# Which queue issues the key and value loads: batch 12's second halves and batch 18 go from GpSimd to SyncE

## The chip, the cores and the metric

The kernel runs on one core of a Trainium2 chip. The metric is device microseconds of one execution. TensorE is called PE here (PEld is its weight load), VectorE DVE, ScalarE ACT, GpSimd POOL and SyncE SP. SP and POOL issue all transfers: what SP issues goes through queue q1, what POOL issues through queue q0, and both run on the same 16 DMA engines.

## The reference

A retention layer (a linear recurrence, 4 batches of 8 heads, 768 steps, head size 64) is followed by a feed-forward layer with squared ReLU.

```
gamma = 1.0 - 2.0 ** (-5.0 - np.arange(H))
for t in range(S):
    state = gamma * state + einsum('bhd,bhe->bhde', k[:, :, t], v[:, :, t])
    y[:, :, t] = scale * einsum('bhd,bhde->bhe', q[:, :, t], state)
x = y.transpose(0, 2, 1, 3).reshape(3072, 512)
h = maximum(x @ w_in, 0)          # 512 -> 2048
out = h * h @ w_out               # 2048 -> 512
```

Inputs and outputs are float32.

## The kernel before

**Chunks.** The 768 steps of a batch are cut into 6 chunks of 128, 24 chunks over all batches. A batch is named by its first chunk: batch 6 is chunks 6 to 11, batch 12 is chunks 12 to 17, batch 18 is chunks 18 to 23. For each chunk the kernel multiplies keys by queries, masks the scores, multiplies them by the values, and carries a state from chunk to chunk. The result of one or more chunks (a block: first four chunks, then two each) is the x of the feed-forward layer, whose two products are most of PE's work.

**The order** is written out by hand. `pieces()` yields the feed-forward products of all blocks, a piece at a time, and after piece n the function `before(n)` emits what `put(n, ...)` has placed there. A place is thus a position in the program, not a time. From chunk 12 on, chunk m ends at place d = 70 + 8 (m - 10), and a place takes about 0.93 us in the profile. Each engine works through its own instructions in this order, so an instruction that waits holds up all behind it on its engine.

**Half form.** Chunks 8 to 23 take a form in which two half chunks lie above each other in the 128 partitions (`attend2`). For chunk m with end d:

- `dma_transpose_q` (L425, place d - 16, even chunks): SP transposes the scaled queries of two chunks by DMA into qT.
- `cast_k2` (L658, place d - 18): POOL casts the keys from the staging tile to ks_bdp.
- `transpose_k2` (L681, place d - 13): SP transposes ks_bdp by DMA into kT. Two kT buffers and two ks_bdp buffers take turns.
- `scale_v2` (L667 on DVE, L675 on POOL, place d - 9): values times a table of decays, kf2.
- `scores2` (L697, place d - 5): PE reads kT and qT. `state2` (L724) and `outputs2` (L746, L753) follow.

The table kf2 and the mask of the half form are made by `pack_constants` in two steps, at places 22 and 38; the second step is two operations of DVE (L202, L203) and one of ACT (L284).

**Loads.** `load_q` (L105) fetches the queries of two chunks, 512 KB, on SP. The keys and values of a whole batch are fetched by `batch_loads` (L147) into a staging tile, 64 partitions, one head and `size` chunks at a time, in runs of 64 floats. Batch 6's rest (chunks 8 to 11) comes by SP in 8 issues of 4 chunks for the keys and 8 for the values, 128 KB each. Batches 12 and 18 come by POOL in 16 issues of 3 chunks each, 96 KB: first the eight head loads of the first three chunks (the first half), then those of the last three (the second half). `places` says at which place each issue stands. Four staging buffers serve all of it; batch 18 takes those of chunks 8 to 11.

**SP's queue** from 78 us on, for every two chunks: kT, kT, two stores of results (L886, L888, which wait for DVE), the query load, qT, and again. The stores' tiles have four buffers.

Of the kernel before, what the change touches and what calls it, by code (L numbers as in the profile page):

```python
# [28 lines left out]
def kernel(  # L29
# [9 lines left out]
    nc = tc.nc  # L39
# [87 lines left out]
    def stage_tile(size):  # L127
        t = stage.tile([P, 2 * NCH * NPAIR * D], FP32, name="stage")
        return t[:, 0:size]
# [3 lines left out]
    def batch_loads(m, name, size):  # L133


        b, i = chunks[m]
        src, to = (k, raw_k) if name == "k" else (v, raw_v)
        t = kept_tiles.pop((m, name), None)
        if t is None:
            t = stage_tile(2 * NCH * NPAIR * D)  # L140
        t = t.rearrange("s (p w d) -> s p w d", p=NPAIR, d=D)
        for j in range(NCH - i):
            to[m + j] = t[:, :, 2 * j : 2 * j + 2].rearrange("s p u d -> s u p d")
        for w in range(0, NCH - i, size):
            for hh, rows in enumerate(halves):
                for p in range(NPAIR):
                    (nc.sync if m == 8 else nc.gpsimd).dma_start(  # L147
                        t[rows, p, 2 * w : 2 * (w + size)],
                        src[b, 2 * p + hh, (i + w) * C : (i + w + size) * C].rearrange(
                            "(w s) d -> s w d", s=64  # L150
                        ),
                    )
                    yield
# [110 lines left out]
    def pack_constants():  # L264
        lng2 = const.tile([P, 2, NPAIR], FP32)
        for hh, rows in enumerate(halves):
            for p in range(NPAIR):
                nc.gpsimd.memset(lng2[rows, :, p : p + 1], float(np.log(gammas[2 * p + hh])))
        logs = lng2.rearrange("s u p -> s (u p)")
        scaled = exponents([[C, NCH], [C // 2, 2], [0, NPAIR]], 1, "ex_k2", logs, halves)  # L270
        nc.gpsimd.memset(cmask2[:], 0.0)
        for rows in halves:
            nc.gpsimd.affine_select(
                out=cmask2[rows],
                in_=cmask2[rows],
                compare_op=ALU.is_gt,
                fill=1.0,
                base=0,
                pattern=[[-1, 2], [-2, C // 4]],
                channel_multiplier=1,  # L280
            )
        yield
        ex = scaled()
        nc.scalar.activation(kf2.rearrange("s i u p -> s i (u p)"), ex[:], AF.Exp, scale=-1.0)  # L284
        yield
# [929 lines left out]
    def put(place, what, *args):  # L1215
        parts.setdefault(place, []).append((what, args))
# [69 lines left out]
        put(place, early_store, tb, which)  # L1286
    packed = pack_constants()
    put(22, next, packed)
    put(38, next, packed)
    for j, t in enumerate(ks_bd2s + v_bd2s + [s_bds[2]]):  # L1290
        for hh in range(2):
            put(24 + j, zero_off_diagonal, t, hh)
# [7 lines left out]
    for m, d in zip(range(PACK_FROM, NCHUNK), done):  # L1300
# [6 lines left out]
        (8, "v"): [33, 33, 34, 34, 35, 35, 36, 36],  # L1307
        (12, "k"): [49, 50, 51, 52, 53, 54, 55, 56] + [74 + j for j in range(8)],
        (12, "v"): [58, 59, 60, 61, 62, 64, 65, 66] + [82 + j for j in range(8)],
        (18, "k"): [92 + 4 * j // 3 for j in range(8)] + [117 + 4 * j // 3 for j in range(8)],  # L1310
        (18, "v"): [103 + 4 * j // 3 for j in range(8)] + [128 + 4 * j // 3 for j in range(8)],
    }
    for (m, name), at_places in places.items():
        loads = batch_loads(m, name, 4 if m == 8 else 3)
        for place in at_places:
            put(place, next, loads)

# [53 lines left out]
```

## Time and profile before

| | us |
|---|---|
| runs shown, median (lowest, highest) | 209.42 (207.17, 210.19) |
| the profiled execution, its own time | 208.36 |
| its span, first to last instruction | 206.6 |
| PE busy | 196.7 |
| DVE busy | 152.9 |
| ACT busy | 135.6 |
| POOL busy | 112.1 |
| POOL's issues at L147, 64 of 662 ns | 42.0 |
| share of 16 DMA engines' time, q1 (SP) and q0 (POOL) | 68.4%, 19.2% |

The table is read from the profile's page: the busy time of an engine is the sum of its instructions in that one execution, and its time outside the span (208.36 - 206.6) is start and end of the program. The share of a queue is the time that its packets took; packets of two queues overlap, so that shares of a stretch can add up to more than one. "Landing" in the views of transfers is the time from the issue to the completion. A line with a start and a duration of SP is the issue, not the transfer.

### The profile page before, as it was taken

How to read it: one execution, taken by the hardware profiler on the slowest of the kernel's cores; microseconds unless marked ns; L12 is line 12 of the kernel's file. 1: busy time of each engine (PE TensorE's matmuls, PEld its weight loads, DVE VectorE, ACT ScalarE, POOL GpSimd, SP SyncE). 2: the span in 40 equal slices, each digit the busy share in tenths (PEclk: the TensorE clock that was granted, in tenths of full speed). 3: DMA queues.
4: the chain of work that ended last, by engine and by line, in shares of the span. 5: the costliest groups of instructions: out<-in, count | busy, mean ns of one | idle time of the engine just before them, and what ended most of it. 6: DMA issues, size and time to landing. Idle time of an engine off the chain costs nothing.

```text
span 206.6 us, 5855 instructions
## 1 busy us (share of the span) xinstructions
PE 196.7 (95%) x2373; PEld 165.2 (80%) x2373; DVE 152.9 (74%) x305; ACT 135.6 (66%) x276; POOL 112.1 (54%) x198
## 2 busy tenths in 40 slices
PE   5889999999999999999999899999999999999993
PEld 1457644876888998789989699999989999898883
DVE  4687899498885678589697588598697797474374
ACT  8375885677943666693794595793785786874730
POOL 5332549823230768975999788779986226100000
PEclk9999999999999999999999999999999999999999
DMA  6999999999999999899699998799897551300202
GB/s 160 290 313 379 310 268 247 205 203 239 238 169 174 240 292 134 149 289 185 174 200 180 221 225 176 190 197 158 217 201 156 137 105 38 119 0 3 102 0 102
DMA packets 70730, 38.12 MB, mean 185 GB/s; under 512 B 43952, under 2 KB 64688, under 8 KB 70704
## 3 DMA queue, kind: packets, MB, share of 16 engines
q1 hardware_dynamic: 65520, 29.37, 68.4%
q0 software_dynamic: 5184, 8.39, 19.2%
q8 instruction: 18, 0.29, 0.6%
q14 instruction: 8, 0.07, 0.1%
HBM read 27.26 MB, written 6.29 MB: 162 GB/s over the span
## 4 chain that ended last, share of the span: by engine, by line
PE 69%; DMA 17%; POOL 4%; DVE 4%; ACT 2%; issue 1%; SPq 0%; DVEq 0%; ACTq 0%
PE psf L803 28%; PE psf L837 12%; PE tp L837 8%; DMA kT<-ks_bdp 7%; PE psf L1096 6%; DMA stage<-in_moe_w_in_dram 4%; DMA w_out_bf<-in_moe_w_out_dram 3%; PE psf L1002 3%; DMA kn<-in_k_dram 3%; POOL stage L147 2%; PE st L697 2%; POOL ks_bdp L658 2%; PE y L753 1%; PE y L746 1%; PE c_ps L724 1%
## 5 line engine op out<-in xcount | busy, mean ns | idle before, releaser
L803 PE MATMUL psf<-xt,w_in_bf 128*128 128x256 bf16 (+2 forms) x880 | 92.5, 259 | 0.4 <-DVE w_in_bf L336 0.3
L803 PEld LDWEIGHTS <-w_in_bf 128*128 128x128 bf16 x880 | 70.9, 98 | 11.2 <-DVE w_in_bf L336 0.7
L812 ACT ACTIVATE h<-psf 128x512 bf16<-128x512 f32 x96 | 56.2, 595 | 20.5 <-PE psf L803 20.0
L774 DVE TENSOR_TENSOR h<-h 128x512 bf16<-128x512 bf16 x72 | 31.8, 458 | 14.8 <-ACT h L812 14.6
L658 POOL CAST ks_bdp<-stage 64x512 bf16<-64x512 f32 x32 | 25.6, 799 | 20.6 <-issue 12.1
L675 POOL COPY v_bd<-v 64x512 bf16<-64x512 bf16 x32 | 20.6, 642 | 23.4 <-DVE v L667 22.2
L837 PEld LDWEIGHTS <-h 128*128 128x128 bf16 x288 | 26.3, 98 | 3.3 <-DVE h L774 0.6
L833 DVE TENSOR_TENSOR osb<-psf,u 128x256 f32<-128x256 f32 x34 | 13.7, 422 | 17.1 <-ACT u L878 9.9
L147 POOL DMA_DIRECT2D stage<-in_k_dram x32 | 21.0, 662 | 0.0
L147 POOL DMA_DIRECT2D stage<-in_v_dram x32 | 21.0, 662 | 0.0
L760 ACT ACTIVATE xt<-y 128x512 bf16<-128x512 f32 x16 | 12.0, 748 | 8.8 <-PE y L753 8.8
L366 DVE TENSOR_TENSOR qs<-qn,qf 128x512 bf16<-128x512 f32 x22 | 16.6, 758 | 1.1 <-DMA qn<-in_q_dram 1.1
L837 PEld LDWEIGHTS <-k_bd 128*128 128x128 bf16 x144 | 13.7, 98 | 1.8 <-issue 0.2
L772 ACT ACTIVATE h<-h 128x512 bf16<-128x512 bf16 x24 | 14.6, 626 | 0.5
L667 DVE TENSOR_TENSOR v<-stage,kf 128x512 bf16<-128x512 f32 x16 | 13.4, 838 | 0.0
L733 ACT ACTIVATE s_bd<-c_ps 64x256 bf16<-64x256 f32 x29 | 10.6, 367 | 3.4 <-PE c_ps L724 3.3
L704 DVE TENSOR_TENSOR pt<-st,cmask 128x512 bf16<-128x512 f32 x16 | 11.0, 687 | 2.4 <-PE st L697 1.9
L734 ACT ACTIVATE s_bd<-c_ps 64x256 bf16<-64x256 f32 x29 | 11.0, 378 | 0.4
L837 PE MATMUL tp<-w_out_bf,h 128*128 128x256 bf16 x72 | 11.2, 273 | 0.0
L334 POOL CAST w_in_bf<-stage 128x256 bf16<-128x256 f32 x14 | 6.1, 465 | 9.2 <-DMA stage<-in_moe_w_in_dram 9.2
L837 PE MATMUL psf<-w_sum,h 128*128 128x256 bf16 x72 | 10.8, 273 | 0.0
L833 DVE TENSOR_TENSOR k_bd<-h 128x512 bf16<-128x512 bf16 x18 | 10.4, 576 | 0.3
(146 smaller groups left out, 328.7 us busy)
## 6 DMA issues: line engine op xcount, KB each, us to landing
qn<-in_q_dram SPq DMA_DIRECT2D x12, 512.0 KB, 7.0
out_dram<-osb SPq DMA_DIRECT2D x23, 256.0 KB, 3.3
stage<-in_k_dram POOLq DMA_DIRECT2D x32, 96.0 KB, 4.5
stage<-in_v_dram POOLq DMA_DIRECT2D x32, 96.0 KB, 4.9
stage<-in_moe_w_in_dram SPq DMA_DIRECT2D x4, 512.0 KB, 6.9
stage<-in_moe_w_in_dram SPq DMA_DIRECT2D x2, 1024.0 KB, 10.9
w_out_bf<-in_moe_w_out_dram POOLq DMA_DIRECT2D x4, 512.0 KB, 9.5
kn<-in_k_dram SPq DMA_DIRECT2D x2, 512.0 KB, 6.4
```

The costliest lines, as they stand in the source:

```text
L147: (nc.sync if m == 8 else nc.gpsimd).dma_start(t[rows, p, 2 * w : 2 * (w + size)], src[b, 2 * p + hh, (i + w) * C : (i + w + size) * C].re ...
L366: engine.tensor_tensor(out=out, in0=by, in1=table[:, :, None].to_broadcast([P, H, D]), op=ALU.mult)
L658: nc.gpsimd.tensor_copy(ks[rows, :, hh, :].rearrange("s (u p) d -> s u p d", u=2), kn[rows])
L667: nc.vector.tensor_tensor(out=v2.rearrange("s (u p) d -> s u p d", u=2), in0=vn, in1=kf2[:, i, :, :, None].to_broadcast([P, 2, NPAIR, D]), ...
L675: nc.gpsimd.tensor_copy(v_bd[rows, :, hh, :], v2[rows])
L772: nc.scalar.activation(hv, hv, AF.Square)
L774: nc.vector.tensor_mul(hv, hv, hv)
L803: nc.tensor.matmul(hp, lhsT=w_in_bf[g][:, cb, fq * 128 : (fq + 1) * 128], rhs=xts[tb][:, cb, cols], start=(cb == 0), stop=(cb == NCB - 1),)
L812: nc.scalar.activation(hv, hp[:], AF.Relu)
L833: nc.vector.tensor_tensor(out=out, in0=in0, in1=in1, op=op)
L837: nc.tensor.matmul(to, lhsT=left[:, j], rhs=right(j) if callable(right) else right[:, j], start=(start and j == 0), stop=(stop and j == NF ...
L1096: nc.tensor.matmul(to[:], lhsT=left(j), rhs=right(j), start=(start and j == 0), stop=(j == NFB // 2 - 1), skip_group_check=True,)
```

## The change

Three edits. First, `batch_loads` now issues on POOL only the first half of batch 12 (w is 0), and all else on SP: the second half of batch 12 (8 loads of keys, 8 of values, 96 KB each, at the places they had) and batch 18. Second, batch 18 is fetched six chunks at a time: 8 loads of keys and 8 of values, 192 KB each, at every second place from 91 (keys) and 102 (values), instead of 32 loads of 96 KB between places 92 and 137. Third, the second step of `pack_constants` stands at place 42 instead of 38.

```diff
-                    (nc.sync if m == 8 else nc.gpsimd).dma_start(
+                    (nc.gpsimd if m == 12 and w == 0 else nc.sync).dma_start(
...
-    put(38, next, packed)
+    put(42, next, packed)
...
-        (18, "k"): [92 + 4 * j // 3 for j in range(8)] + [117 + 4 * j // 3 for j in range(8)],
-        (18, "v"): [103 + 4 * j // 3 for j in range(8)] + [128 + 4 * j // 3 for j in range(8)],
+        (18, "k"): [91 + 2 * j for j in range(8)],
+        (18, "v"): [102 + 2 * j for j in range(8)],
...
-        loads = batch_loads(m, name, 4 if m == 8 else 3)
+        loads = batch_loads(m, name, {8: 4, 12: 3, 18: 6}[m])
```

In the instruction order, POOL has 48 issues less and SP 32 more. On SP, seven key loads of batch 12 stand between kT 12 and kT 13; one key load and five value loads of it between kT 13 and qT 14, among two stores and the query load; three value loads between qT 14 and kT 14; one value load of batch 12 and three key loads of batch 18 between kT 14 and kT 15; three loads of batch 18 between kT 15 and qT 16, three between qT 16 and kT 16, five between kT 16 and kT 17, and the last two after kT 17. PE's instructions are the same, in the same order; on DVE and ACT only the table's three operations move.

## The prediction

> **What bounds the kernel now.** I read the engine shares first, then the waits of PE (TensorE), then the busy time stage by stage, then SP's (SyncE's) own queue and the landing time of single transfers.
>
> ```profile
> PE 196.7 (95%) x2373; PEld 165.2 (80%) x2373; DVE 152.9 (74%) x305; ACT 135.6 (66%) x276; POOL 112.1 (54%) x198
> ```
>
> PE is busy 196.7 of 206.6 us, so only its 9.9 idle us can be won by moving transfers. The stages say where they lie (columns: PE, PEld, DVE, ACT, POOL busy, granted clock, DMA share, GB/s):
>
> ```profile
> 60.00:75.00 15.00, 14.89 (x223) 13.82 (x221) 10.16 (x21) 9.15 (x21) 5.30 (x9) 1.00 1.09 224
> 75.00:90.00 15.00, 14.47 (x191) 12.86 (x189) 10.40 (x21) 10.59 (x23) 13.07 (x20) 1.00 1.08 182
> 90.00:105.00 15.00, 15.00 (x186) 13.40 (x182) 12.26 (x22) 10.19 (x22) 12.44 (x19) 1.00 1.02 203
> 105.00:120.00 15.00, 13.96 (x171) 12.18 (x168) 10.76 (x21) 9.65 (x22) 13.67 (x21) 1.00 1.17 197
> 120.00:135.00 15.00, 15.00 (x187) 13.63 (x185) 11.88 (x23) 10.99 (x24) 12.21 (x19) 1.00 0.92 204
> ```
>
> Between 60 and 135 us PE idles 0.11 + 0.53 + 0 + 1.04 + 0 us, at the full clock; the rest lies in the prologue and the tail, which the change does not reach. PE's waits name the cause of almost all of it: the score products wait for the transposed keys kT, twice, 0.5 us for chunk 10 and 1.0 us for chunk 14. POOL (GpSimd) is 54% busy and PE waits for it nowhere after the prologue.
>
> ```profile
> PE st L697 <- DMA kT<-ks_bdp: 1.5, 2, 1.0
> ```
>
> The long one in SP's queue, and what a transpose takes there:
>
> ```profile
> 102.24 0.43 SPq L105 DMA_DIRECT2D qn<-in_q_dram  x1
> 103.97 1.83 SPq L425 DMA_TRANSPOSE qT<-qs  x1
> 105.96 3.42 SPq L681 DMA_TRANSPOSE kT<-ks_bdp  x1
> ```
>
> kT of chunk 14 goes out at 105.96, right behind its qT, and the chain of waits ends at 115.47, 9.46 us later. Its landing time beside a POOL load, and that of a kT right behind qT, a query load and the eight 128 KB loads that SP issues already today (from 55.32 us):
>
> ```profile
> stage<-in_v_dram POOLq DMA_DIRECT2D x1, 96.0 KB, 6.7
> qT<-qs SPq DMA_TRANSPOSE x1, 7.9
> kT<-ks_bdp SPq DMA_TRANSPOSE x1, 9.5
> ```
>
> ```profile
> qT<-qs SPq DMA_TRANSPOSE x1, 5.8
> kT<-ks_bdp SPq DMA_TRANSPOSE x1, 5.0
> ```
>
> The bound is PE. What the change can touch on the path are two kT waits, and the slack of the other kT transposes.
>
> **The change, part by part.**
>
> *POOL gives up 48 issues.* Batch 12's second halves (16) and batch 18 (32) go, at 662 ns each: 31.8 us, of POOL's 112.1. None of it is on PE's path. It brings POOL's casts forward, and with them the issue of kT for odd chunks (kT 15 goes out at 112.62, as its cast ends). Those have slack already: kT 15 lands 4.7 us later and is used at 124.6. Worth 0. Kept on the range: at most the 0.5 us wait of chunk 10, which I leave, because the POOL loads ahead of its cast (75.54, 1.26 us in the chain) are first halves, and these stay on POOL.
>
> *SP gains 32 issues:* 16 of 96 KB, 16 of 192 KB. A 128 KB load costs SP 633 ns (median); I take 0.63 us for 96 KB and, for 192 KB, 0.63 to 0.95 (half as many runs again). No row shows that size. The eight loads from 55.32 took 6.27 us to issue and landed in a steady 5.0 to 4.9 us, so the queue takes 128 KB in 0.78 us without falling behind; by size 96 KB is 0.59 and 192 KB 1.18 us of queue.
>
> The new order on SP puts loads in front of transposes. In turn:
>
> - kT 13 (94.86 before): seven 96 KB loads in front, 7 x 0.63 = 4.4 us behind kT 12's issue (92.2 + 2.0): about 98.7, plus 5.0 to 6.8 lands at 103.7 to 105.5. Used at 108.4. Hidden.
> - Query load, then qT 14: six loads and two stores in front. From 98.7 + 1.3 the six loads (3.8) and two stores (0.33 each) end at 104.4; before, qT 14 started at 103.97, because its scaling on DVE ended at 103.94. So 0 to 0.5 us late.
> - kT 14: three 96 KB loads now lie between qT 14 and kT 14, 3 x 0.63 = 1.9 us. Issue at 105.96 + 1.9 = 107.9. PE wants it at 115.47 - 1.02 = 114.45, so 6.5 us are left. Landing is bounded by 3.1 (kT 19, alone) and 9.5 (this one today). I take 5.0 to 5.8, since after the change the transfers in front are what they are in the row of 65.6 us: SP loads, a query load, qT. Lands at about 113.5: the wait goes, **-1.02 us**. Bounds: -1.02 to +1.9 (9.5 us again).
> - kT 15: four loads in front of it after kT 14, issue about 112.5, as before; up to 9.5 us would still beat 124.6. Hidden.
> - kT 16: three 192 KB loads between qT 16 (ends 121.96) and kT 16: 1.9 to 2.85 us. Issue at 123.9 to 124.8 instead of 122.14; PE wants it at 130.3, so 5.5 to 6.4 us are left, and today it takes 6.3. Three loads are 576 KB in front; in the row with 5.0 it was 1 MB and more. I take 5.4: **0**, by a hair. Bounds: 0 to +4.0 (9.5 us).
> - kT 17: five 192 KB loads in front, issue 126 + 5 x 0.95 = 130.8, plus 6.7 is 137.5; used at 139.6. kT 18: nothing new between qT 18 and it; 137.04 + 6.7 = 143.7, used at 145.2, as today. From there on SP issues no load at all and POOL none either; PE had no waits there, so 0.
>
> Of the loads' own users: batch 12's last key half goes out behind kT 13 (about 100, wanted by the cast at 110.70), batch 18's last key load behind kT 16 (about 126, lands at 131, wanted by the cast at 133.71), its last value load behind the stores at 133.1 (lands at 138.5, wanted at 142.15). Hidden by 5, 2.5 and 3.5 us. The stores get up to 2 us later; the four output buffers hide that.
>
> *Price for the DMA engines.* POOL's packets: 401 took 25.6% of 16 engines in 15 us, 153 ns for 2.1 KB; SP's in 55 to 62 us: 4906 took 103.1% in 7 us, 23.5 ns for 0.27 KB. Per byte SP's are dearer by a fifth, so the 4.7 MB moved cost some 26 us of all 16 engines instead of 21. Off the path unless a backlog stands in front of kT 16, which is the slow rival.
>
> The Trainium skill, "DMA: Bandwidth & Descriptors", section "Why small descriptors are slow (HBM only)", puts the overhead of an unpacked 256-byte packet at 27%; the rows give about 20%. By either figure the sum above stays as it is.
>
> *The table of the half form*, place 38 to 42: ACT waited 2.49 us for DVE at 59.95 and PE lost 0.11 us in that stage. Two DVE operations (0.48, 0.65) and one of ACT (0.24) come a little later; the table is first read at 67.13 by the value scaling of chunk 8. Bounds -0.11 to +0.5 (half a us of DVE in front of that scaling); taken as 0.
>
> **Sum.** -1.02 + 0 + 0 on the profiled execution's 208.36 us (span 206.6 and 1.76 around it): 207.3. The median of the runs shown is 209.42, 1.06 above that execution; the four times (207.17, 208.36, 209.42, 210.19) have a mean of 208.8, and I apply the sum to that: **207.8 us**. A measurement of this kernel tells about 2%, 4.2 us, from no change.
>
> **Rivals.**
>
> 1. *The wait only changes its cause (no gain).* kT 14 lands as late as now, because the same bytes are in the engines between 98 and 110 us, or 1.9 us of later issue eat up the quicker landing. For it: POOL's loads themselves landed slowly there (6.7), so the engines and not the queue may be full. Against: SP starts batch 12's halves at 94, while POOL issued nothing from 95.4 to 98.8. Landing of 7.5 instead of 5.4 gives back the 1.0: 208.8 to 209.4.
> 2. *Slower: kT 16 behind batch 18.* From 109.5 to 124.8 SP hands its queue ten 192 KB loads (10 x 1.18 = 11.8 us), kT 15, qT 16 and kT 16 (about 1.5 each, from the 3 us of full engines that qT and kT take alone at 166.5), a query load (1.75 at 300 GB/s) and two stores (1.4): 19.5 us of work, so it is done at 129 plus the backlog at 109.5, and about 1.2 us go by until it is seen. With no backlog it is on time (130.2); from 0.1 us of backlog on, PE waits. Four us of backlog, about what kT 14's 9.5 us stand for, cost 4 us, less the 1.0 won: 209 to 212.4.
>    In the Trainium skill, "DMA: Bandwidth & Descriptors", section "Queues, rings and completion order", an engine alternates between queue rows packet by packet. By that rule a transpose loses its separate turn once the loads share its row, which is this rival; the trace agrees in so far as kT 14 took its 9.5 us even with a row apart from the loads, and no run here shows batch 18 in one row yet.
> 3. *The move does nothing, since all of it is hidden.* kT 14's wait differs by execution (the runs spread from 207.17 to 210.19) and neither kernel meets it on average: 208.4 to 209.4, inside rival 1's band.
>
> **Chances.** Wait gone, nothing new: 0.50 (206.4 to 208.8). Rivals 1 and 3: 0.22 (208.4 to 209.4). Rival 2: 0.23 (209 to 212.4, and in 0.05 of it more than 4 us). Something larger on SP, as a full queue that stops its issues: 0.05. The range leaves out the upper part of the last two and a little below: 206.2 to 211.2. Faster by over 2% would need 205.2, below the 206.8 that is left of 208.36 without any kT wait: 0.02. Slower by over 2%, 213.6: 0.08. Within: 0.90.
>
> **What the profile after would show.** POOL at about 80 us busy, its queue at some 2,800 packets instead of 5,184, and none of its issues at L147 after 90 us; SP's queue at about 84,000 packets. If right: no wait at the score products between 105 and 120 us (PE 15.00), and kT 14 and 16 landing in under 6.5 us. Rival 1: the wait is still there at chunk 14. Rival 2: a wait of PE for kT between 120 and 135 us, with kT 16 issued after 124 and landing in 6 us or more. Wrong altogether: SP's loads taking 2 us or more to issue, or POOL's cast of chunk 18 waiting for its load after 133.

## The result, and the profile after

The changed kernel ("after" below) takes 214.39 us (median of 6 runs, 213.09 to 216.15) against 209.04 us (6 runs, 207.17 to 210.19) for the kernel before ("before"): ratio **1.030**, 95% interval 1.025 to 1.034. Ratios, here and below, leave out runs that took over 1.5% more than the fastest run of their kernel. It is slower; 207.8 was forecast, 206.2 to 211.2 as the range, and a chance of 0.08 was given to a slowdown of over 2%. All profile lines below are of single profiled executions; after's took 215.44 us, with a span of 213.3.

The first line of the page, and PE's longest wait:

```profile
PE 198.5 (93%) x2369; PEld 166.6 (78%) x2373; DVE 152.2 (71%) x305; ACT 135.8 (64%) x276; POOL 80.1 (38%) x150
```

```profile
PE st L697 <- DMA kT<-ks_bdp: 6.2, 3, 3.9
```

The span grew by 6.7 us. The wait for kT grew from 1.5 to 6.2, which is 4.7 of it, and PE's busy time by 1.8: together 6.5. Of the 4.7, 3.9 are a new wait at chunk 16. Another 0.9 is at chunk 10, where PE waited 1.4 us instead of 0.5, at 85 us and so before the first moved load goes out at 94.75. That wait lies between 0 and 1.8 us in the profiled executions of this document, whatever the edit, and no run ties it to the change. The stages say where (PE, PEld, DVE, ACT, POOL busy, granted clock, DMA share, GB/s):

```profile
75.00:90.00 15.00, 13.51 (x177) 11.98 (x175) 9.90 (x21) 9.65 (x21) 12.14 (x19) 1.00 1.01 192
90.00:105.00 15.00, 14.78 (x179) 13.02 (x178) 11.57 (x22) 9.79 (x22) 6.75 (x10) 1.00 0.84 184
105.00:120.00 15.00, 14.13 (x174) 12.54 (x172) 11.06 (x21) 10.01 (x21) 5.02 (x8) 1.00 1.02 182
120.00:135.00 15.00, 11.64 (x145) 10.33 (x143) 9.80 (x18) 9.29 (x21) 5.60 (x8) 1.00 1.28 202
```

The stage from 105 us has the wait for kT 14 still (0.9 us); that from 120 us, in which PE idled nowhere before, has the long one, for kT 16. There the DMA share is 1.28 instead of 0.92, at about the same GB/s. Finer windows show the other 1.8 us:

```profile
132.00:135.00 3.00, 0.00 (x0) 0.00 (x0) 0.00 (x0) 0.34 (x1) 0.00 (x0) 1.00 1.32 154
135.00:136.00 1.00, 0.44 (x9) 0.44 (x10) 0.00 (x0) 0.00 (x0) 0.00 (x0) 0.74 1.26 208
136.00:138.00 2.00, 2.00 (x14) 1.45 (x12) 1.03 (x2) 0.08 (x1) 0.00 (x0) 0.50 1.35 167
138.00:139.00 1.00, 1.00 (x7) 0.71 (x6) 0.00 (x0) 0.97 (x2) 0.00 (x0) 0.55 1.36 164
139.00:141.00 2.00, 2.00 (x23) 1.81 (x22) 1.17 (x3) 0.95 (x3) 0.57 (x1) 1.00 1.38 159
```

PE stands idle until 135.5, and then runs at about half its clock for 3 us: with the 1.8 us of busy time, the wait of 3.9 us costs over 5.

SP's queue in front of kT 16 (start, duration of the issue):

```profile
122.55 0.43 SPq L105 DMA_DIRECT2D qn<-in_q_dram  x1
123.02 1.40 SPq L147 DMA_DIRECT2D stage<-in_k_dram  x1
124.53 3.00 SPq L425 DMA_TRANSPOSE qT<-qs  x1
127.57 0.62 SPq L147 DMA_DIRECT2D stage<-in_v_dram  x1
128.24 0.65 SPq L147 DMA_DIRECT2D stage<-in_k_dram  x1
128.93 0.66 SPq L147 DMA_DIRECT2D stage<-in_v_dram  x1
129.70 3.40 SPq L681 DMA_TRANSPOSE kT<-ks_bdp  x1
```

Each row starts where the one before it ends: SP has no break. The queries that qT 16 transposes were scaled by 121.66 (DVE's last operation on them starts at 120.57 and takes 1.09; before, 119.54 and 1.09). So kT 16 starts 8.0 us behind the scaling, where it was 1.5 us (122.14 against 120.63). Of these 6.5 us more, 2.8 are the late start of qT 16, 1.7 its longer issue (3.00 instead of 1.30) and 2.1 the three loads behind it. In the chain of waits it then lands in 5.82 us, where it was 6.3; the row of kT 14 stands above it:

```profile
112.96 3.48 DMA kT<-ks_bdp
129.70 5.82 DMA kT<-ks_bdp
```

### The profile page after: what moved, and what is told of

Its sections match the earlier page's. It is cut to its first block, busy times and chain, and to the rows that moved or that the text cites. A ratio compares the mean times of both kernels' runs of the same rounds, so it can differ in the third digit from the quotient of the medians.

```text
span 213.3 us, 5833 instructions
## 1 busy us (share of the span) xinstructions
PE 198.5 (93%) x2369; PEld 166.6 (78%) x2373; DVE 152.2 (71%) x305; ACT 135.8 (64%) x276; POOL 80.1 (38%) x150
## 4 chain that ended last, share of the span: by engine, by line
PE 70%; DMA 10%; DVE 8%; ACT 4%; issue 3%; POOL 3%; SPq 0%; DVEq 0%
PE psf L803 31%; PE psf L837 11%; DMA kT<-ks_bdp 8%; PE tp L837 7%; PE psf L1096 6%; PE psf L1002 3%; DMA kn<-in_k_dram 3%; DVE h L774 2%; PE st L697 2%; ACT h L812 2%; POOL ks_bdp L658 1%; PE y L753 1%; PE y L746 1%; PE c_ps L724 1%; ACT h L772 1%
## 5 line engine op out<-in xcount | busy, mean ns | idle before, releaser
L774 DVE TENSOR_TENSOR h<-h 128x512 bf16<-128x512 bf16 x72 | 33.3, 478 | 15.4 <-ACT h L812 15.2
L658 POOL CAST ks_bdp<-stage 64x512 bf16<-64x512 f32 x32 | 24.5, 767 | 51.1 <-issue 24.2
L667 DVE TENSOR_TENSOR v<-stage,kf 128x512 bf16<-128x512 f32 x16 | 12.6, 785 | 0.0
L697 PE MATMUL st<-qT,kT 128*128 128x64 bf16 x128 | 6.6, 196 | 6.2 <-DMA kT<-ks_bdp 6.2
L697 PEld LDWEIGHTS <-kT 128*128 128x128 bf16 x128 | 5.7, 100 | 7.3 <-DMA kT<-ks_bdp 7.1
L837 PE MATMUL tp<-w_out_bf,h 128*128 128x256 bf16 x72 | 11.2, 273 | 0.2 <-DVE h L774 0.2
L837 PE MATMUL psf<-w_sum,k_bd 128*128 128x256 bf16 x80 | 10.4, 273 | 0.0
```

Source lines behind the costliest of these rows:

```text
L658: nc.gpsimd.tensor_copy(ks[rows, :, hh, :].rearrange("s (u p) d -> s u p d", u=2), kn[rows])
L667: nc.vector.tensor_tensor(out=v2.rearrange("s (u p) d -> s u p d", u=2), in0=vn, in1=kf2[:, i, :, :, None].to_broadcast([P, 2, NPAIR, D]), ...
L697: nc.tensor.matmul(st[:, c, :], lhsT=kT[:, c, :], rhs=half_of(a["qT"], p, u), start=True, stop=True,)
L774: nc.vector.tensor_mul(hv, hv, hv)
L837: nc.tensor.matmul(to, lhsT=left[:, j], rhs=right(j) if callable(right) else right[:, j], start=(start and j == 0), stop=(stop and j == NF ...
```

## The experiments

Two theories at first. **A**: SP's own time. Every issue costs SP some 0.65 us, the queue is in order, so kT goes out too late. **B**: the DMA engines. They get too many bytes in front of kT. Ratios are to the kernel before, with 95% intervals; for one part of a kernel's extra time I add its waits for kT in its one profiled execution (1.5 us before). Experiment 1 shows how far these differ between executions.

### 1. The table's second step alone

```diff
-    put(38, next, packed)
+    put(42, next, packed)
```

> The kernel before with the table's second step at place 42 alone. By the prediction 0: ratio 0.998 to 1.003. The three profiles with the table at 42 showed PE waiting 1.3 to 1.9 us between 75 and 90 us, those with the table at 38 0.4 to 1.0; if that is the table's doing and not chance, ratio 1.003 to 1.007 and a wait at chunk 10 above 1 us.

Measured: 1.001 (0.997 to 1.004). The table's place costs nothing. Its profiled execution took 212.07 us, against a median of 208.64, and waited for kT more than the kernel before did:

```profile
PE st L697 <- DMA kT<-ks_bdp: 3.7, 3, 2.5
```

The 2.5 us are at chunk 14, with no load moved. So the waits of one profiled execution tell where PE stood, and a difference of 1 to 2 us between two of them is not yet the price of an edit; the ratios tell that.

### 2. Batch 12's second halves alone

The kernel before, with this edit only:

```diff
-                    (nc.sync if m == 8 else nc.gpsimd).dma_start(
+                    (nc.sync if m == 8 or (m == 12 and w > 0) else nc.gpsimd).dma_start(
```

> Only batch 12's second halves go to SyncE; batch 18 stays on GpSimd in 32 issues of 96 KB, and the table stays at place 38. Theory A (SyncE's own issue time: what stands ahead of a transpose in SyncE's queue delays its issue): SyncE is busy without a break from about 94 to 114 us only, kT of chunk 16 goes out as in the kernel before (about 1.5 us after its qT could start), PE waits about 1 us for chunk 14 and not for chunk 16; ratio to before 0.995 to 1.01. Theory B (the DMA engines' backlog: packets of 256 bytes are a fifth dearer per byte, wherever they stand): kT of chunk 14 lands later than its 9.5 us, the wait at chunk 14 grows to 2 us; ratio 1.00 to 1.01 as well, so here the wait tells, not the time.

Measured: 1.021 (1.017 to 1.025), waits for kT 3.6 us, the longest 2.9 at chunk 14. These bytes are handed over at the same places as before. SP's queue there:

```profile
107.05 0.75 SPq L147 DMA_DIRECT2D stage<-in_v_dram  x1
107.89 3.07 SPq L425 DMA_TRANSPOSE qT<-qs  x1
111.01 1.95 SPq L147 DMA_DIRECT2D stage<-in_v_dram  x3
113.07 1.27 SPq L681 DMA_TRANSPOSE kT<-ks_bdp  x1
```

It is the picture of after: loads ahead of qT 14, qT slow to issue, three loads, and kT 14 at 113 instead of 106. It landed in 5.28 us, so it came late by its issue, as A says, and not by a landing above 9.5 us, as B says; the ratio is above both forecasts. At chunk 16, where this version has no load on SP, PE did not wait. Of the 5.1 us by which this execution's span is longer, 1.5 is a longer wait for w_out at 36 us (below), so what the halves themselves cost is known less well than the ratio.

### 3. Issues without bytes

The kernel before, all real loads on GpSimd as they were, and 32 loads of 1 KB issued by SP at the places where the change puts its loads (their tile is read by nothing):

```diff
+    def tiny_load(j):
+        nc.sync.dma_start(tiny[:, j], k[0, 0, 0:64, 0:4])
...
+    for j, place in enumerate(tiny_at):
+        put(place, tiny_load, j)
```

> The kernel before (all its loads on GpSimd) with 32 tiny extra loads of 1 KB in all 64 partitions, issued by SyncE at the places of the 32 moved loads; they fill a spare tile that nothing reads. Issues without bytes. Theory A in its plain form (each issue costs SyncE a fixed 0.6 us): qT 16 and kT 16 go out 4 us late or more, PE waits at chunk 16, ratio 1.01 to 1.02. Theory A in its other form (an issue of SyncE is long because its queue is full, so bytes and issues act together): the tiny issues take 0.35 us or less, kT 14 and 16 go out at most 1.5 us later, ratio 1.000 to 1.005. Theory B: no bytes, no change, 1.00.

Measured: 1.024 (1.020 to 1.028), waits for kT 4.0 us in three, the longest 1.5.

```profile
96.19 5.04 SPq L1321 DMA_DIRECT2D tiny<-in_k_dram  x7
101.33 1.25 SPq L681 DMA_TRANSPOSE kT<-ks_bdp  x1
...
107.90 2.62 SPq L425 DMA_TRANSPOSE qT<-qs  x1
110.57 1.86 SPq L1321 DMA_DIRECT2D tiny<-in_k_dram  x3
112.54 1.25 SPq L681 DMA_TRANSPOSE kT<-ks_bdp  x1
```

Seven issues of 1 KB take SP 5.04 us, 0.72 each. kT 14 is at 112.54, almost where the real loads put it. So the issues alone, with hardly a byte, make kT go out late: theory A holds for this part. Its cost was put at 1 to 2%. Of the 3.9 us by which this execution's span is longer, 1.1 is a wait for w_out at 36 us (below) and 0.8 the wait at chunk 10, both in front of the first of these issues; the waits for kT 14 and kT 16 are longer by 0.5 and 1.2. That the issues cost the whole 2.4% is thus not shown.

### 4. Batch 18 alone

The kernel before, with batch 18 on SP in six-chunk issues at the new places, batch 12 on GpSimd:

```diff
+                    (nc.gpsimd if m == 12 else nc.sync).dma_start(
...
+        (18, "k"): [91 + 2 * j for j in range(8)],
+        (18, "v"): [102 + 2 * j for j in range(8)],
...
+        loads = batch_loads(m, name, {8: 4, 12: 3, 18: 6}[m])
```

> Only batch 18 goes to SyncE, six chunks an issue, at the changed places; batch 12 stays on GpSimd; table at 38. Theory A: SyncE has no old load to work off when batch 18 begins at 109 us, so qT 16 starts at most 1 us late instead of 2.8; the three loads behind it still cost 2 us; kT 16 is late by 0 to 2 us; ratio 1.00 to 1.012. Theory B: batch 18's 3.1 MB are the heavy part, the wait at chunk 16 stays near 3.9 us; ratio 1.02 to 1.03.

Measured: 1.024 (1.021 to 1.028), waits for kT 6.2 us, the longest 3.8 at chunk 16, as in after. That is B's figure and above A's. But kT 16 landed in 6.08 us; it was late because it went out at 130.44, from an SP without a break. The issue of kT 15 ahead of it took 5.17 us, against 1.23 before, so SP was held up by more than a fixed price for each issue.

### 5. The changed kernel, no load between an even chunk's qT and kT

```diff
-        (12, "v"): [58, 59, 60, 61, 62, 64, 65, 66] + [82 + j for j in range(8)],
-        (18, "k"): [91 + 2 * j for j in range(8)],
-        (18, "v"): [102 + 2 * j for j in range(8)],
+        (12, "v"): [58, 59, 60, 61, 62, 64, 65, 66] + [89 + j for j in range(8)],
+        (18, "k"): [89, 91, 93, 95, 105, 106, 107, 108],
+        (18, "v"): [105 + j for j in range(8)],
```

> All loads of the change stay on SyncE with the same sizes, but none stands between a kT of an odd chunk and the next kT of an even chunk: batch 12's value halves at places 89 to 96 and batch 18's loads at 89 to 95 and 105 to 112, right behind kT 14 and kT 16. Theory A: qT and kT of chunks 14 and 16 go out as soon as DVE has scaled the queries; no wait at 14 or 16, only chunk 10's 0.5 to 1.4 us; ratio 0.99 to 1.00. Theory B: the same bytes, packed closer; kT 16 or the next ones land in 8 us and more, and PE waits 3 us or more somewhere between 105 and 150 us; ratio 1.015 or more.

Measured: 1.026 (1.021 to 1.031). PE waited no more at chunks 14 and 16, as A says, but the time is B's (1.015 or more, with a wait of 3 us somewhere): kT 17 now stood behind twelve loads, went out at 140.21, and PE waited 3.1 us for it.

### 6. The changed kernel, three loads moved behind kT 16

```diff
-        (18, "k"): [91 + 2 * j for j in range(8)],
-        (18, "v"): [102 + 2 * j for j in range(8)],
+        (18, "k"): [91, 93, 95, 97, 99, 101, 105, 105],
+        (18, "v"): [105, 105] + [106 + 2 * j for j in range(6)],
```

> The changed kernel with only the three 192 KB loads that stood between qT 16 and kT 16 moved behind kT 16. Theory A: kT 16 is issued 3 x 0.66 + 0.2 = 2.2 us sooner, at about 127.5 us, lands 5.8 later at 133.3, wanted at 131.6: PE's wait there falls from 3.9 to about 1.7 us, the granted clock stays at 0.9 or more behind it, and of the two the run gains 2.2 + 1.6 us: ratio 1.01 (1.004 to 1.018). kT 17 may stand behind more loads and wait for up to 2 us, which would give 1.02. Theory B: the bytes that were handed over before are the same, kT 16 lands at about 135 all the same: wait 3 to 4 us, ratio 1.025 to 1.035.

Measured: 1.033 (1.029 to 1.037). kT 16 was issued at 126.40, 3.3 us sooner than in after, and PE waited 0.5 for it; then 2.9 for kT 17:

```profile
126.40 1.25 SPq L681 DMA_TRANSPOSE kT<-ks_bdp  x1
127.70 1.31 SPq L147 DMA_DIRECT2D stage<-in_k_dram  x2
129.06 7.33 SPq L147 DMA_DIRECT2D stage<-in_v_dram  x6
136.50 2.70 SPq L681 DMA_TRANSPOSE kT<-ks_bdp  x1
```

Moving a load only chooses which kT pays; the ratio is in B's range (1.025 to 1.035). And six issues took 7.33 us, 1.22 each, against 0.72 of the tiny ones: SP itself is held up here. The DMA share from 130 to 135 us is 1.36. But that share alone does not tell when SP is held up: in after it was 1.34 from 128 to 130 us, where loads of the same size took 0.65 and 0.66.

### 7. Batch 18 in twice as many issues

```diff
-        (18, "k"): [91 + 2 * j for j in range(8)],
-        (18, "v"): [102 + 2 * j for j in range(8)],
+        (18, "k"): [91 + 2 * (j // 2) for j in range(16)],
+        (18, "v"): [102 + 2 * (j // 2) for j in range(16)],
...
-        loads = batch_loads(m, name, {8: 4, 12: 3, 18: 6}[m])
+        loads = batch_loads(m, name, {8: 4, 12: 3, 18: 3}[m])
```

> As the changed kernel, but batch 18 in 32 issues of three chunks (96 KB), two at each of its places: the same bytes in the same stretch of the order, twice the issues. Theory A: ten to twelve more issues of 0.6 us stand ahead of kT 16, which goes out 5 to 7 us later still; PE waits 9 us or more at chunk 16, the clock drops for longer; ratio 1.05 or more. Theory B: the same bytes, the same backlog: wait about 4 us, ratio 1.03.

Measured: 1.044 (1.040 to 1.048), two runs; waits for kT 8.4 us, the longest 6.3. Sixteen issues more for the same bytes make it worse than B had it (1.03, a wait of about 4 us), and by less than A had it (1.05 or more, 9 us).

### 8. The moved loads on ScalarE

The changed kernel, with its moved loads issued by ScalarE:

```diff
+                    (nc.gpsimd if m == 12 and w == 0 else nc.sync if m == 8 else nc.scalar).dma_start(
```

> The changed kernel with its 32 moved loads issued by ScalarE instead of SyncE: the same sizes, places and kind of packets on the same 16 engines, in a hardware queue of their own, so SyncE issues what it issued before. Theory A (SyncE's issue time, with its queue strictly in order): qT and kT go out as in the kernel before; PE waits for kT only at chunk 10 and 14, at most 2.5 us in sum; but 32 issues of 0.6 us now hold up ScalarE's own work, so the time may still be 1.00 to 1.03 of before, with PE waiting for other things. Theory B (the bytes in the engines): the transposes land late all the same, 8 us and more, and PE waits for kT 5 us or more in sum.

Measured: 1.045 (1.038 to 1.052). The waits for kT are all but gone, but ACT now stands in its own issues:

```profile
PE tp L837 <- ACT u L868: 3.3, 2, 2.9
PE psf L803 <- ACT xt L760: 2.4, 2, 1.8
PE tp L837 <- ACT u L861: 1.3, 2, 0.7
PE st L697 <- DMA kT<-ks_bdp: 0.3, 1, 0.3
```

This does not refute B, as I first thought: kT 14 and kT 16 landed in 9.38 and 9.20 us, the 8 us and more that B forecast (before: 9.46 and 6.3), but PE, held up by ACT for some 7 us, came later to them.

### 9. Batch 18 in six-chunk issues, on GpSimd

The places and the size of experiment 4, the engine of the kernel before.

> The kernel before with one edit: batch 18 in 16 issues of six chunks at the changed places, still issued by GpSimd; SyncE untouched, batch 12 untouched, table at 38. Theory A: GpSimd gives up 16 issues (10.6 us), SyncE nothing more to do, so no new wait: ratio 0.992 to 1.003. Theory B: batch 18's bytes are now in half the stretch, from 109 to 133 us, and delay kT 16 and 18: PE waits 1 to 3 us there, ratio 1.005 to 1.02.

Measured: 1.026 (1.019 to 1.032). SP's instructions are those of the kernel before, and yet PE waited for kT. (The profiled execution, 220.31 us, was far above this kernel's median of 215.59, so its wait of 11.6 us for kT 16 tells the place and not the size.) The ratio is above theory A's range, 0.992 to 1.003: A alone fails here.

### 10 and 11. Batch 18 behind the even kT only

At most six loads of 192 KB in 15 us, each right behind an even chunk's kT; SP has time for all of it. Once on SP (as in experiment 4), once on GpSimd:

```diff
+        (18, "k"): [73 + j for j in range(6)] + [89, 90],
+        (18, "v"): [91, 92, 93, 94, 105, 106, 107, 108],
```

> The kernel before, with batch 18 alone on SyncE in its 16 issues of 192 KB, but never more than six in 15 us, and each of them between the kT of an even chunk and that of the odd one after it: six behind kT 12, six behind kT 14, four behind kT 16. Batch 12 stays on GpSimd. Theory A (SyncE's own time is the bound): for every two chunks SP now has 4.8 us of transposes, stores and query load and 6 x 0.65 = 3.9 us of loads, 8.7 of 14.9 us, and nothing in front of an even kT. The odd kT go out 3 to 4 us later and land by 104, 119 and 134 us, before they are wanted. So no wait of PE for kT beyond those of the kernel before (together 1 to 2 us), ratio 0.99 to 1.005. Theory B (the bytes of SyncE's loads in the DMA engines): the same 3.1 MB in the same queue as in the run with batch 18 alone, so a wait of 2 us or more at a chunk from 13 to 17, ratio 1.01 to 1.03.

> The kernel before, with batch 18 on GpSimd in 16 issues of 192 KB at the places of the spread version (six behind kT 12, six behind kT 14, four behind kT 16), so that SyncE's instructions are those of the kernel before and only the queue differs from the spread version. Theory A alone (SyncE's time): SP is untouched, no new wait, ratio 0.99 to 1.005. Theory B as the run with batch 18 in six-chunk issues on GpSimd showed it (dense loads through q0 take the engines from q1's transposes): six loads are 1.2 MB at once, 1.2 MB at 200 GB/s are 6 us, so the next kT lands in 10 us or more, a wait of 2 us or more for it, ratio 1.01 to 1.025.

Measured: 1.044 (1.039 to 1.049) on SP, 1.059 (1.053 to 1.065) on GpSimd. I had taken the first for a version that might beat both kernels. SP's queue of it:

```profile
95.65 7.63 SPq L147 DMA_DIRECT2D stage<-in_k_dram  x6
103.39 3.94 SPq L681 DMA_TRANSPOSE kT<-ks_bdp  x1
107.43 0.54 SPq L886 DMA_DIRECT2D out_dram<-osb  x1
108.07 0.98 SPq L888 DMA_DIRECT2D out_dram<-osb  x1
109.10 0.44 SPq L105 DMA_DIRECT2D qn<-in_q_dram  x1
109.63 6.25 SPq L425 DMA_TRANSPOSE qT<-qs  x1
115.98 4.16 SPq L681 DMA_TRANSPOSE kT<-ks_bdp  x1
```

Few issues, and SP is full all the same: 1.27 us a load, 3.94 and 4.16 a kT, 6.25 a qT. On GpSimd, PE's waits for kT came to 10.3 us with no SP instruction touched, and the kT it waited for landed in 8.62 and 12.52 us. So B acts too, and more than it was given (1.01 to 1.03 and 1.01 to 1.025); theory A's sum of 0.65 us pieces does not hold in such a stretch, with a DMA share of 1.25 to 1.45 in the first from 94 to 104 us.

### 12 and 13. Who issues, or when

Both are the kernel before with 96 KB issues. In the first, batch 18's 32 loads stay at their old places and only go to SP:

```diff
-                    (nc.sync if m == 8 else nc.gpsimd).dma_start(
+                    (nc.gpsimd if m == 12 else nc.sync).dma_start(
```

> The kernel before, with batch 18 issued by SyncE in the same 32 issues of 96 KB at the same places as before: only the engine that issues changes, no byte is handed over earlier. Theory A (each issue costs SP about 0.65 us and the transposes stand behind it): 32 issues more between 105 and 150 us are 20.8 us in 42; two loads stand between qT 16 and kT 16 and two between qT 18 and kT 18, and qT itself starts up to 2 us later, so kT 16 or kT 18 is 2 to 4 us later and PE waits 1 to 3 us: ratio 1.005 to 1.02. Theory B (too many bytes at once): the bytes come when they came before, no wait beyond those of before, ratio 0.995 to 1.005.

In the second they stay on GpSimd and only come early, two at each new place:

```diff
+        (18, "k"): [91 + 2 * (j // 2) for j in range(16)],
+        (18, "v"): [102 + 2 * (j // 2) for j in range(16)],
```

> The kernel before, with batch 18 on GpSimd in its 32 issues of 96 KB, but two at each of the 16 new places, so that all 3.1 MB are handed over between places 91 and 116 instead of 92 and 137. SyncE's instructions are untouched. Theory B (too many bytes at once, whoever issues them): as with six-chunk issues on GpSimd, the share of the DMA engines goes over 1.15 between 105 and 135 us and kT lands in 10 us or more, PE waits 3 us or more for it, ratio 1.015 to 1.035. Theory A (SyncE's time alone): no new wait, 0.995 to 1.005. A third reading, that it is the 192 KB issue and not the early hand-over that holds the transposes up, gives 0.995 to 1.005 too.

Measured: **1.002 (0.998 to 1.006)** for the engine alone, **1.050 (1.041 to 1.059)** for the early hand-over alone, the second above the 1.015 to 1.035 of B. So for batch 18 the change of engine costs nothing at the old pace, and the early hand-over costs as much or more without it; the larger issue is not needed for that. The transfers issued between 119 and 135 us landed so, in the kernel before, in the first and in the second:

```profile
stage<-in_v_dram POOLq DMA_DIRECT2D x8, 96.0 KB, 3.9
stage<-in_k_dram POOLq DMA_DIRECT2D x2, 96.0 KB, 4.4
kT<-ks_bdp SPq DMA_TRANSPOSE x2, 4.8
```

```profile
stage<-in_v_dram SPq DMA_DIRECT2D x8, 96.0 KB, 3.5
stage<-in_k_dram SPq DMA_DIRECT2D x2, 96.0 KB, 4.6
kT<-ks_bdp SPq DMA_TRANSPOSE x2, 3.5
```

```profile
stage<-in_k_dram POOLq DMA_DIRECT2D x8, 96.0 KB, 8.1
stage<-in_v_dram POOLq DMA_DIRECT2D x6, 96.0 KB, 8.4
qT<-qs SPq DMA_TRANSPOSE x1, 8.3
kT<-ks_bdp SPq DMA_TRANSPOSE x1, 11.6
```

SP can carry batch 18 at the old pace for nothing, though it has no break there from 104.73 to 135.90 us. Handed over early, the same loads on GpSimd double their landing, from 3.9 and 4.4 us before, and take kT 16 from 6.3 (4.8 is the median of two kT) to 11.6, without SP doing anything more. The clock fell here as well: 0.50 from 134 to 138 us, behind a wait of 3.9 us.

### 14. A still more even pace

If pace is all, the kernel before should lose its own wait of 1.0 us for kT 14 when batch 12's last value loads and batch 18's come more evenly, on GpSimd:

```diff
+        (12, "v"): [58, 59, 60, 61, 62, 64, 65, 66] + [83 + 2 * j for j in range(8)],
+        (18, "k"): [98 + 5 * j // 4 for j in range(8)] + [118 + 5 * j // 4 for j in range(8)],
+        (18, "v"): [108 + 5 * j // 4 for j in range(8)] + [128 + 5 * j // 4 for j in range(8)],
```

> The kernel before with the same 96 KB issues on GpSimd, more evenly spaced: batch 12's last eight value loads at every second place from 83 (83 to 97 instead of 82 to 89), batch 18's 32 at 0.8 a place from 98 to 136 (instead of 0.75 from 92 to 137, behind batch 12's 16 in 16 places). If the pace of the loads in front of a transpose sets when kT lands, less stands in front of kT 14 and the kernel before's own wait of 1.0 us there goes: ratio 0.993 (0.988 to 0.999). If SyncE's own order is what counts, or the wait is set by the query load and qT alone, nothing changes: 0.997 to 1.005. If the later loads are late for the casts or the scaling of batch 18, POOL or DVE waits for them behind place 116 and the ratio goes over 1.005.

Measured: 1.005 (1.001 to 1.009), and kT 14 took 9.85 us to land, and PE waited 1.5 us for it. But little was thinned out in front of it: GpSimd issued 6 loads from 98 to 106 us, against 8, and queue q0 moved 0.63 MB there, against 0.59. The forecast gain did not come, and whether the loads make that wait stays open. No version tried beats the kernel before.

## Why the prediction was wrong

The wait came where rival 2 has it, at chunk 16, and the time went past rival 2's range, 209 to 212.4. The step that failed is **"kT 16 ... I take 5.4: 0, by a hair"**, and of it the issue time, "123.9 to 124.8", which is 3.3 to 4.2 us behind the scaling's end at 120.63; it was 8.0 us behind it. The step added the three loads behind qT 16 (1.9 to 2.85 us forecast, 2.1 measured) and let qT 16 itself go out and end as before; that it started 2.8 us late and took 1.7 us longer was put at nothing. PE waited 3.9 us in place of 0. The landing, 5.82 us against 5.4, was sized about right.

Point by point:

- *POOL.* Forecast about 80 us busy and 2,800 packets; 80.1 and 2,880. Worth 0, as said: right, and no help.
- *The price of an issue.* 0.63 us for 96 KB, 0.63 to 0.95 for 192 KB; the medians of the 32 moved loads are 0.64 (keys) and 0.62 (values), both sizes mixed, the longest 1.51. Right for most loads by themselves. What was missing is the total: I priced each gap by the loads in it and never added up SP's time. From 105 to 120 us its rows in the timeline sum to 14.2 of 15 us, in a stretch without breaks from 94.75 to 142. In such a queue what delays kT 13 delays qT 14, and so on. That alone need not cost anything: in experiment 12 SP has no break for 31 us either.
- *The transposes' own issue* was left at 1.3 to 1.8 us. In after it took 3.8 (qT 14), 3.0 (qT 16) and 3.4 (kT 16). The prediction's own rows had a 3.42, for kT 14, with no load of keys or values in SP's queue there.
- *kT 14*, the sum's -1.02. Issue forecast at 107.9, measured 112.96; landing forecast 5.4, measured 3.48. The first error is 5.1 us to the bad, the second 1.9 to the good, and PE itself came some 1.1 us later, at 115.6: 0.9 us of wait instead of none, against 1.0 before. The gain did not come.
- *The DMA engines.* "Off the path unless a backlog stands in front of kT 16" names the right place, and rival 2 prices it by the work in SP's queue alone. A sum over both queues could have been made from rows of the kernel before: SP's queue, without any load of keys or values, moved 2.04 MB from 90 to 105 us.

```profile
q1 hardware_dynamic: 4712, 2.04, 78.8%
```

  That is 136 GB/s. Batch 18's 3.15 MB over 45 places of 0.93 us add 75: 211 GB/s. Over 25 places they add 135: 271. After 75 us no stage of 15 us in any of these runs moved more than 231. A six-chunk issue brings the second half of the batch 21 to 26 places earlier than before (keys at 91 to 105 instead of 117 to 126), and that early hand-over is what cost the time in experiment 13. That the rate is why is argued, not shown: from 119 to 135 us of experiment 13 the engines moved 177 GB/s at a DMA share of 1.15, against 203 at 0.94 before, so they moved less and not as much as ever they could.
- *Rival 2's argument*, that a transpose loses its separate turn once the loads share its queue, is not borne out for batch 18: in experiment 12 they share it and cost nothing, in experiment 13 they do not and cost 5.0%. That kT 14 took 9.5 us with the loads in the other queue spoke against it from the start. Its sign, a landing of kT 16 in 6 us or more, just failed too: the delay was in the issue. And its sum counts ten loads of 192 KB in front of kT 16; they are nine, and one of 96 KB, 11.2 us and not 11.8.
- *The table:* 0, right (experiment 1).
- *The clock* was not in the working at all: the 1.8 us of busy time that PE gained are, but for some 0.2, the half-speed stretch behind the long wait (1.6 us lost from 135 to 139 at the clocks shown).

By parts, batch 12's halves alone cost 2.1% and batch 18 alone 2.4%, together 3.0%: not a sum. Batch 12's come at the same places as before, 16 in 16 places, and what the traces show there is SP's order and time: kT 14 goes out late with or without bytes (experiments 2 and 3). That this is the whole of the 2.1% is argued, since PE also waited 2.5 us at chunk 14 in an execution without a moved load (experiment 1). Batch 18's cost comes from its hand-over early, on GpSimd (13) and on SP (4, there with the larger issues), and not from the engine (12). The number of issues does not set the cost: 32 more on SP cost 0.2% in experiment 12 and 2.4% in experiment 3, at other places and with GpSimd's loads kept.

What stays open: how much of kT 16's 8.0 us is SP's fixed time and how much is SP held up by full engines, since both show as longer issues; and what holds SP up, the engines or the length of its own queue, which the prediction had as a chance of 0.05. And a wait for w_out at 36 us, 0.2 us in the profiled execution of the kernel before, was 1.7, 1.3 and 2.0 in those of experiments 2, 3 and 5, whose instructions up to there are the old ones. It makes up to 1.8 us of those single spans; whether it hangs on the program or on the execution was not tried.

## What to carry to other kernels

Before moving transfers to another engine's queue, add up that queue's whole time per period, transposes and stores with it, and see what stands behind each new issue: in a queue with no breaks, whatever delays one transfer is handed on to the next, and a transfer that PE waits for has only its slack against it. Then add up bytes per us for the stage, old and new, against what the engines have moved in that kernel: fewer, larger loads at fewer places bring the last of their bytes earlier, and in this kernel the early hand-over delayed the others on either queue. A gap that "just" fits in the working has a price on the far side: in the seven profiled executions with a longest wait for kT of 2.9 to 4.2 us (after, experiments 2, 4, 5, 6, 10 and 13), PE's busy time was 1.2 to 3.7 us above the 196.7 of before, which I put down to the clock.

## What the runs showed of the hardware

- **An issue on SP costs about the same for 1 KB as for 192 KB** where nothing holds SP up: 0.72 each (seven of 1 KB), 0.62 to 0.66 (192 KB, after). In some stretches with a DMA share of 1.2 to 1.4 it is longer, for loads (1.22 to 1.27), kT (3.9 to 4.2) and qT (6.25), but not in all: the rows with 0.65 and 0.66 are from such a stretch too. The Trainium skill, "DMA: Bandwidth & Descriptors", section "Issuing engines are not separate DMA queues", says that all transfers run on the same 16 engines whoever issues them, and that the time to initiate one is usually small beside the transfer. Experiments 12 and 13 agree with the first. The rows of experiment 3 agree with the second, with medians of 0.59 us for an issue of 1 KB and 4.4 to its landing; but a small time adds up in SP's order, and kT 14 went out at 112.54 instead of 105.96.
- **The granted clock after a wait.** Behind waits of 3.9 us (after, experiment 13), 4.2 (experiment 10) and 2.9 (experiment 2) it stood at 0.50 for 2 to 4 us; behind 1.0 (before) and 1.5 (experiment 3) it stayed at 1.00. In between, the length of the wait alone does not decide: behind 2.5 us (experiment 1, 118 to 120 us) it was 0.50, behind 2.7 (experiment 11, 102 to 110 us) 1.00. Experiment 2, from 116 us on:

```profile
116.00:118.00 2.00, 0.00 (x0) 0.00 (x0) 0.00 (x0) 0.19 (x1) 2.00 (x4) 1.00 1.30 176
118.00:120.00 2.00, 1.61 (x18) 1.31 (x19) 1.02 (x2) 0.00 (x0) 0.78 (x2) 0.81 1.16 263
120.00:122.00 2.00, 2.00 (x11) 1.45 (x10) 0.28 (x1) 1.23 (x2) 0.00 (x0) 0.50 0.70 206
```

  The Trainium skill, "TensorE: Matmul & The Clock Gate", section "Why this matters for your kernels", asks for no idle gaps above about 3 us between matmul bursts. The traces agree, with 2.9 us, and once 2.5, already enough.
